# A fused state-space and gated feed-forward layer: x tile 0 loaded as two halves, the second chunk's x in one transfer, and the up projection's column halves in one stretch

## The chip, the core and the metric

The kernel runs on one core of one Trainium2 chip. The metric is device time in microseconds, taken over several runs of the same program. The core's engines run side by side, each on its own list of instructions, and wait for each other on semaphores: TensorE (PE; its weight loads are PEld), VectorE (DVE), ScalarE (ACT), GpSimd (POOL) and SyncE (SP). Here SP, ACT and POOL also issue the transfers (DMAs); SPq and ACTq in the profile are their issues.

## The reference

x has 2048 tokens of 512 features, in bfloat16. One layer norm feeds two branches, and everything is added:

```
xn = layernorm(x)
A: Bu = xn @ B_bar.T                      (complex, 512 states)
   h[t] = Lam_bar * h[t-1] + Bu[t]
   a = 2 * Re(h @ C.T) + xn * Dskip
B: b = (silu(xn @ w_gate) * (xn @ w_up)) @ w_down      (inner width 1376)
out = x + a + b
```

Lam_bar and B_bar follow from Lambda, log_dt and B, which are small vectors and two 512x512 matrices.

## The kernel before

**Tiling.** The tokens go in 16 tiles of 128, in four chunks of 512 (`NCH` = 4, `TPC` = 4 tiles per chunk). `xall` holds x, `xnT` the normalized x with features on the partitions, which is what the matmuls read. The inner width 1376 is ten full blocks of 128 (`FT - 1`) and a last one of 96. For each chunk there are gate and up matmuls (`gateup_tile`, line 432), the projection to the states (`bproj_tile`, line 357), the recurrence on DVE (`ssm_ops`: rotate u by tables, scan at line 399, rotate back into `wt`), and the output (`out_chunk`): for each tile of tokens one PSUM bank collects eleven feed-forward matmuls (`out_ffn`, line 513) and eight state matmuls (`out_ssm`, line 522). ACT moves PSUM to SBUF. There are eight PSUM banks.

**Order.** The order on each engine is the order of the program text. TensorE's order is written out at the end of the function; the work of DVE is kept in a list, `backlog`, of pieces with costs. `pump(us)` issues pieces as TensorE's time goes by, and `need(tag)` issues what is left of a tag before TensorE uses it. `multiply` issues the products silu(gate) x up (line 451). Chunk 0 begins in a head that works tile by tile (`head_mm`, line 605), after nine dummy matmuls (line 582); then bproj of chunk 0, the rest of its gate and up, bproj 1, gate/up 1, bproj 2, output 0, gate/up 2, bproj 3, output 1, gate/up 3, output 2, output 3.

**The head.** Tile 0 of x is loaded from SP (line 123), tile 1 from ACT (line 125, after a memset of the same bytes, line 124), tile 2 from SP (128), tile 3 from ACT (129), with the first groups of `wg` and `wu` between them (`load_w1`, line 112). The second chunk's x follows from SP in two transfers of two tiles (137). For each tile DVE takes statistics (lines 185, 186; for tiles 1 and 3 lines 612 and 627), ACT makes the inverse deviation (190, 191), DVE normalizes (203), TensorE transposes (220), and DVE or ACT copies the result into `xnT` (227, 229). Before tile 0 is normalized, DVE takes the statistics of tile 1; before tile 2 is normalized, those of tile 3.

**Later layer norms.** `ln_rest(c, on_act)` gives the pieces for chunk c: four statistics, a power on POOL (195), a small product nb on DVE (198), four normalizations (for chunks 2 and 3 on ACT, line 208), each followed by a transposing DMA from SP (234). For chunk 3 the normalized tile is `xn_end`.

**The last block of 96.** Its gate columns and 32 of its up columns form one matmul of 128 columns (`w_last`, line 458, 96 gate and 32 up). The other 64 up columns (`wu_last`) fill half the columns of the array, so two chunks run side by side: for each of four k, a matmul into the upper and one into the lower half of a bank (line 468). This is done for chunks 0 and 1 in gate/up 1, and for chunks 2 and 3 in gate/up 3. ACT copies the halves to `ul` (471), and a product fills `gu_last` (473), of which there are two buffers.

**Output.** For chunks 0 to 2 ACT copies a bank to `res` (529) and POOL adds it to the output in memory (530). Before that SP copies x of these chunks to the output (734). `skip_op` and `skip_store` (490, 496) add xn x Dskip.

Of the kernel before, what the change touches and what calls it, by code (L numbers as in the profile page):

```python
# [11 lines left out]
BF16 = mybir.dt.bfloat16  # L12
ALU = mybir.AluOpType
ACT = mybir.ActivationFunctionType
# [9 lines left out]
def kernel(  # L24
# [17 lines left out]
    nc = tc.nc  # L42
    _, L, D = A_x.shape
# [15 lines left out]
    LA, LB = 32, 64  # L59
# [13 lines left out]
    def bank(shape=(128, CW), dtype=F32):  # L73
        return psum.tile(list(shape), dtype, name="ps")
# [4 lines left out]
    x_v = A_x[0].rearrange("(n p) d -> p n d", p=128)  # L79
    out_v = out[0].rearrange("(n p) d -> p n d", p=128)  # L80
# [4 lines left out]
    xall = const.tile([128, NT, D], BF16, name="xall")  # L85
    xnT = const.tile([128, KD, L], BF16, name="xnT")
# [8 lines left out]
    wu_last = const.tile([128, KD, LB], BF16, name="wu_last")  # L95
    wd_sb = const.tile([128, FT, D], BF16, name="wd_sb")
# [5 lines left out]
    CF = const.tile([128, 2, NQ, D], BF16, name="CF")  # L102
# [7 lines left out]
    def load_w1(q, tiles, view, gi):  # L110
        a, b = fgroups[gi]
        q.dma_start(out=tiles[gi][:], in_=view[:, :, a * 128:min(F, b * 128)])
# [6 lines left out]

    nc.scalar.preload_act_table_set("natural_log_exp_and_others")  # L120


    nc.sync.dma_start(out=xall[:, 0, :], in_=x_v[:, 0, :])
    nc.vector.memset(xall[:, 1, 0:D // 2], 0.0)
    nc.scalar.dma_start(out=xall[:, 1, :], in_=x_v[:, 1, :])
    load_w1(nc.sync, wg_g, wg_v, 0)
    load_w1(nc.scalar, wu_g, wu_v, 0)
# [37 lines left out]

    gu_last = [const.tile([128, CW], BF16, name=f"gu_last{i}") for i in range(2)]
    for t in (gu_last[0][LB + LA:128, :], gu_last[1][LB + LA:128, :], wd_sb[LB + LA:128, FT - 1, :]):
        nc.vector.memset(t, 0.0)  # L170


# [74 lines left out]
    V = nc.vector  # L247
# [177 lines left out]
    gu_tiles = {}  # L425
    u_pair = {}
    products = []
# [24 lines left out]

    up_last = {}

    def gateup_last(c):
        ps = bank()
        for k in range(KD):
            nc.tensor.matmul(ps[:], lhsT=w_last[:, k, :], rhs=xnT[:, k, c * CW:(c + 1) * CW],  # L458
                             start=(k == 0), stop=(k == KD - 1))
        u = up_last[c] = up_p.tile([128, CW], BF16, name="ul", bufs=2)  # L460
        nc.scalar.activation(out=gu_last[c % 2][0:LB + LA, :], in_=ps[0:LB + LA], func=ACT.Silu)
        nc.scalar.copy(out=u[LB:LB + LA, :], in_=ps[LB + LA:128])
        if c % 2 == 0:
            return
        ps = bank()
        for k in range(KD):
            for i in range(2):
                nc.tensor.matmul(ps[i * LB:(i + 1) * LB], lhsT=wu_last[:, k, :],  # L468
                                 rhs=xnT[:, k, (c - 1 + i) * CW:(c + i) * CW], start=(k == 0), stop=(k == KD - 1))
# [29 lines left out]
    o_tiles = {}  # L499

    def out_blocks(n):

        return ((0, D // 2), (D // 2, D - 128), (D - 128, D)) if n == NT - 1 else ((0, D),)

    def out_ffn(n):
        c, i = divmod(n, TPC)
        o_tiles[n] = []
        for lo, hi in out_blocks(n):
            o = bank((128, hi - lo))
            o_tiles[n].append(o)  # L510
            for fi in range(FT):
                t = gu_last[c % 2] if fi == FT - 1 else gu_tiles[c][:, fi, :]
                nc.tensor.matmul(o[:], lhsT=t[:, i * 128:(i + 1) * 128], rhs=wd_sb[:, fi, lo:hi],  # L513
                                 start=(fi == 0), stop=False)

    def out_ssm(n):
        c, i = divmod(n, TPC)
        res = opool.tile([128, D], BF16, name="res")
        for o, (lo, hi) in zip(o_tiles[n], out_blocks(n)):
            for part in range(2):  # L520
                for q in range(NQ):
                    nc.tensor.matmul(o[:], lhsT=w_tiles[c][:, part, q, i * 128:(i + 1) * 128],  # L522
                                     rhs=CF[:, part, q, lo:hi], start=False, stop=(part == 1 and q == NQ - 1))
            if c == NCH - 1:
                V.tensor_tensor(out=res[:, lo:hi], in0=o[:], in1=xn_end[:, i, lo:hi], op=ALU.add)  # L525
                for a, b in ((0, D // 2), (D // 2, D)) if i == 0 else ((lo, hi),):
                    (nc.sync if b == D else nc.scalar).dma_start(out=out_v[:, n, a:b], in_=res[:, a:b])
            else:
                nc.scalar.copy(out=res[:, lo:hi], in_=o[:])  # L529
                nc.gpsimd.dma_start(out=out_v[:, n, lo:hi], in_=res[:, lo:hi], accum_op=ALU.add)  # L530

# [52 lines left out]
    def ln_rest(c, on_act):  # L584
        ops = [(0.7, lambda n=n: ln_stats(n)) for n in range(c * TPC, (c + 1) * TPC)]
        def fin():
            ln_rstd(c * TPC, (c + 1) * TPC)
        def nbf():
            ln_nb(c * TPC, (c + 1) * TPC)
        ops += [(0.1, fin)]  # L590
        tail = [(0.1, nbf)] if on_act else []
        for n in range(c * TPC, (c + 1) * TPC):
            def one(n=n):
                (norm_act if on_act else norm_dve)(n)
                xT_dma(n)
            tail.append((0.05 if on_act else 0.35, one))
        return ops, tail
# [88 lines left out]
    def spread(ops, others, tag, tag2):  # L686

        others = list(others)
        for op in ops:
            queue(tag, [op])  # L690
            if others:
                queue(tag2, [others.pop(0)])

    def queue_ssm(c):
        fwd, back = ssm_ops(c)
# [46 lines left out]
    queue_ssm(3)  # L742
    out_chunk(1)
    gateup_chunk(3)
    out_chunk(2)
    need("skip")
    out_chunk(3)
# [30 lines left out]
```

## Time and profile before

| | |
|---|---|
| runs | 179.62 us median of 3 (179.45 to 179.9) |
| profiled execution | 179.41 us, span 177.6 us |
| granted TensorE clock | 1.0 |
| transfers in all | 15.53 MB, mean 87 GB/s |
| in slices of 4.44 us, the first five | 157, 320, 265, 234, 146 GB/s |
| line 432, gate and up | 37.6 and 37.5 us of TensorE |
| line 513, feed-forward output | 37.2 us |
| line 357 and line 522 | 28.2 and 28.1 us |
| line 468, the 64-column halves | 16 matmuls, 2.1 us |

The span is the time from the first to the last instruction of the program; the profiled execution's own time is 1.8 us more. Busy time of a matmul is modelled and overlaps that of the next, so the spacing of starts says more than the mean of one. The largest single waits of other engines are those of POOL for results (87.2 us) and of ACT for output banks (38.4 us), which is idle time of engines that TensorE does not wait for at that point. Some transfers of the head, from issue to landing: x tiles 0 and 1 took 2.1 and 2.3 us, x tiles 2 and 3 4.5 us each, the first groups of wg and wu 3.9 and 4.6 us, their second groups 4.9 and 5.0 us, and the two transfers of the second chunk's x 5.2 and 4.1 us.

### The profile page before, as it was taken

To read this page: it belongs to the slowest core of one execution; us is meant where nothing else is said; L and a number is where in the kernel's file an instruction comes from. 1 tells how busy PE (TensorE), PEld (TensorE's weight loads), DVE (VectorE), ACT (ScalarE), POOL (GpSimd) and SP (SyncE) were. 2 spreads that over 40 slices of the span, in tenths; PEclk is the share of its full clock that TensorE was granted. 3 is DMA by queue.
4 is the path that set the end of the run, shared out by engine and by line. 5 is a ranking of instruction groups with operands and counts; after the bars stand their busy time and mean duration, and the time that the engine had idled before them with its cause. 6 is when DMAs were issued, how large, how long until landed. Compare 5 with 4: busy or idle time off the path is not lost.

```text
span 177.6 us, 2450 instructions
## 1 busy us (share of the span) xinstructions
PE 172.7 (97%) x900; PEld 83.1 (47%) x916; DVE 154.2 (87%) x237; ACT 94.3 (53%) x173; POOL 23.2 (13%) x29
## 2 busy tenths in 40 slices
PE   8999999999999999999999999999999999999993
PEld 2784444444444444444444444444444444444743
DVE  6789997999999999999999999999999999940033
ACT  4589696978499965033997660024866600220000
POOL 6003000001300000029000000013505000150000
PEclk9999999999999999999999999999999999999999
DMA  5998948993146400022820000007276900072012
GB/s 157 320 265 234 146 95 232 350 140 89 30 87 208 181 0 0 0 30 29 122 61 0 0 0 0 4 2 85 30 119 94 147 0 0 0 87 32 4 49 69
DMA packets 29131, 15.53 MB, mean 87 GB/s; under 512 B 18848, under 2 KB 29056, under 8 KB 29088
## 3 DMA queue, kind: packets, MB, share of 16 engines
q1 hardware_dynamic: 24416, 11.41, 28.3%
q0 software_dynamic: 3456, 3.28, 13.9%
q10 hardware_dynamic: 1248, 0.69, 1.4%
q8 instruction: 7, 0.11, 0.3%
q14 instruction: 4, 0.03, 0.1%
HBM read 8.03 MB, written 5.24 MB: 75 GB/s over the span
## 4 chain that ended last, share of the span: by engine, by line
PE 95%; DVE 1%; DMA 1%; issue 1%
PE ps L432 36%; PE ps L513 21%; PE ps L357 15%; PE ps L522 15%; PE ps L605 3%; PE ps L458 2%; DMA xall<-in_A_x_dram 1%; PE ps L468 1%; PE ps L220 1%; DVE stats L185 0%; DVE stats L612 0%; DVE xall L203 0%; DVE res L525 0%; PE ps L582 0%; DVE mv L186 0%
## 5 line engine op out<-in xcount | busy, mean ns | idle before, releaser
L432 PE MATMUL ps<-xnT,wg 128*128 128x512 bf16 x143 | 37.6, 379 | 0.3
L432 PE MATMUL ps<-xnT,wu 128*128 128x512 bf16 x146 | 37.5, 379 | 0.1
L513 PE MATMUL ps<-wd_sb,guT 128*128 128x512 bf16 (+2 forms) x177 | 37.2, 355 | 0.2
L399 DVE TENSOR_TENSOR_SCAN g<-r_t,car,u 128x512 bf16<-128x512 f32 x24 | 28.9, 1266 | 0.0
L522 PE MATMUL ps<-CF,wt 128*128 128x512 bf16 (+2 forms) x140 | 28.1, 355 | 0.2
L357 PE MATMUL ps<-xnT,BT 128*128 128x512 bf16 x126 | 28.2, 379 | 0.1
L529 ACT CAST res<-ps 128x512 bf16<-128x512 f32 x12 | 7.0, 585 | 38.4 <-PE ps L522 38.4
L446 ACT ACTIVATE guT<-ps 128x512 bf16<-128x512 f32 x40 | 24.8, 620 | 3.8 <-PE ps L432 3.7
L447 ACT CAST u<-ps 128x512 bf16<-128x512 f32 x40 | 24.2, 604 | 4.1 <-PE ps L432 4.0
L513 PEld LDWEIGHTS <-guT 128*128 128x128 bf16 x180 | 16.9, 98 | 18.0
L432 PEld LDWEIGHTS <-wu 128*128 128x128 bf16 x148 | 14.5, 98 | 17.5
L432 PEld LDWEIGHTS <-wg 128*128 128x128 bf16 x148 | 14.3, 98 | 17.6 <-issue 0.8
L530 POOL DMA_DIRECT2D out_dram<-res x12 | 11.1, 998 | 87.2 <-ACT res L529 87.2
L522 PEld LDWEIGHTS <-wt 128*128 128x128 bf16 x144 | 13.5, 98 | 14.2
L357 PEld LDWEIGHTS <-BT 128*128 128x128 bf16 x128 | 12.5, 98 | 15.1
L359 ACT CAST u<-ps 128x512 bf16<-128x512 f32 x32 | 17.5, 589 | 3.1 <-PE ps L357 3.0
L525 DVE TENSOR_TENSOR res<-ps,xn_end 128x512 bf16<-128x512 f32 (+2 forms) x6 | 3.0, 514 | 14.5 <-PE ps L522 14.5
L451 DVE TENSOR_TENSOR guT<-guT,u 128x1024 bf16<-128x1024 bf16 x20 | 13.5, 680 | 0.0
L367 DVE TENSOR_TENSOR pm<-u,c 128x2048 bf16<-128x2048 bf16 x8 | 9.8, 1221 | 1.2 <-ACT c L284 1.1
L195 POOL TENSOR_TENSOR rstd<-ve,neg_half 128x4 f32<-128x4 f32 x3 | 5.2, 1749 | 40.2 <-DVE ve L194 40.2
L185 DVE BATCH_NORM_STATS2 stats<-xall 128x6 f32<-128x512 bf16 x14 | 9.4, 671 | 1.1 <-DMA xall<-in_A_x_dram 1.1
L367 DVE TENSOR_TENSOR pm<-g,c 128x2048 bf16<-128x2048 bf16 x8 | 9.7, 1218 | 0.1
(108 smaller groups left out, 166.1 us busy)
## 6 DMA issues: line engine op xcount, KB each, us to landing
out_dram<-in_A_x_dram SPq DMA_DIRECT2D x1, 1536.0 KB, 8.9
out_dram<-res POOLq DMA_DIRECT2D x12, 128.0 KB, 3.1
out_dram<-xall POOLq DMA_DIRECT2D x3, 512.0 KB, 5.7
wd_sb<-in_B_w_down_dram SPq DMA_DIRECT2D x1, 1280.0 KB, 10.3
xall<-in_A_x_dram SPq DMA_DIRECT2D x1, 1024.0 KB, 6.3
xall<-in_A_x_dram SPq DMA_DIRECT2D x2, 256.0 KB, 4.6
wg<-in_B_w_gate_dram SPq DMA_DIRECT2D x1, 512.0 KB, 5.2
wu<-in_B_w_up_dram SPq DMA_DIRECT2D x1, 512.0 KB, 6.1
```

Source lines behind the costliest of these rows:

```text
L185: nc.vector.bn_stats(out=stats[:, n, :], in_=xall[:, n, :])
L357: nc.tensor.matmul(ps[:], lhsT=BT[:, part, k, q * 128:(q + 1) * 128], rhs=xnT[:, k, c * CW:(c + 1) * CW], start=(k == 0), stop=(k == KD - 1))
L359: nc.scalar.copy(out=u_tiles[c][:, part, q, :], in_=ps[:])
L367: V.tensor_tensor(out=t[:], in0=flat(src()[:, i]), in1=flat(tab[:]), op=ALU.mult)
L399: V.tensor_tensor_scan(out=g()[:, part, q, :], data0=r_t[:, q:q + 1].to_broadcast([128, CW]), data1=u_tiles[c][:, part, q, :], initial=ini ...
L432: nc.tensor.matmul(ps[:fs, lo:hi], lhsT=wslice(groups, fi, k), rhs=xnT[:, k, c * CW + lo:c * CW + hi], start=(k == 0), stop=(k == KD - 1))
L446: nc.scalar.activation(out=guT[:fs, fi, :], in_=psg[:fs], func=ACT.Silu)
L447: nc.scalar.copy(out=u_pair[c][:fs, fi % 2, :], in_=psu[:fs])
L451: products.append(lambda: V.tensor_tensor(out=g, in0=g, in1=u, op=ALU.mult))
L513: nc.tensor.matmul(o[:], lhsT=t[:, i * 128:(i + 1) * 128], rhs=wd_sb[:, fi, lo:hi], start=(fi == 0), stop=False)
L522: nc.tensor.matmul(o[:], lhsT=w_tiles[c][:, part, q, i * 128:(i + 1) * 128], rhs=CF[:, part, q, lo:hi], start=False, stop=(part == 1 and q ...
L530: nc.gpsimd.dma_start(out=out_v[:, n, lo:hi], in_=res[:, lo:hi], accum_op=ALU.add)
```

## The change

x tile 0 is loaded as two halves of 64 tokens, one from SP and one from ACT; the memset ahead of tile 1 goes. The second chunk's x comes in one transfer. The 64 up columns of the last block are done for all four chunks in one stretch, `up_halves`, which stands in the output of chunk 0, behind its ten feed-forward matmuls per tile. For this the layer norm of chunk 3 moves ahead, among the pieces of chunk 0's recurrence (`spread` now takes a list of tags), and `need("ln3")` stands before the stretch. The eleventh feed-forward matmul of chunk 0's tiles (`out_last`) then needs a product that is not there yet, so it is done in `out_end`, in gate/up 2, after its block 0, and the four result copies and accumulations of chunk 0 (`out_leave`) go with it. `gu_last` gets a third buffer and `ul` has four.

```diff
-    nc.sync.dma_start(out=xall[:, 0, :], in_=x_v[:, 0, :])
-    nc.vector.memset(xall[:, 1, 0:D // 2], 0.0)
+    nc.sync.dma_start(out=xall[0:64, 0, :], in_=x_v[0:64, 0, :])
+    nc.scalar.dma_start(out=xall[64:128, 0, :], in_=x_v[64:128, 0, :])
     nc.scalar.dma_start(out=xall[:, 1, :], in_=x_v[:, 1, :])
...
-    for n in (TPC, TPC + 2):
-        nc.sync.dma_start(out=xall[:, n:n + 2, :], in_=x_v[:, n:n + 2, :])
+    nc.sync.dma_start(out=xall[:, TPC:2 * TPC, :], in_=x_v[:, TPC:2 * TPC, :])
...
+    def product_last(c):
+        g, u = gu_last[c % 3][0:LB + LA, :], ul(c)[0:LB + LA, :]
+        products.append(lambda: V.tensor_tensor(out=g, in0=g, in1=u, op=ALU.mult))
+
+    def up_halves():
+        pss = []
+        for c in range(0, NCH, 2):
+            ps = bank()
+            pss.append(ps)
+            for k in range(KD):
+                for i in range(2):
+                    nc.tensor.matmul(ps[i * LB:(i + 1) * LB], lhsT=wu_last[:, k, :],
+                                     rhs=xnT[:, k, (c + i) * CW:(c + i + 1) * CW], start=(k == 0), stop=(k == KD - 1))
+        for c in range(NCH):
+            i = c % 2
+            nc.scalar.copy(out=ul(c)[0:LB, :], in_=pss[c // 2][i * LB:(i + 1) * LB])
+        product_last(0)
+        product_last(1)
...
-        if c % 2 == 0:
-            return
-        ps = bank()
-        for k in range(KD):
-            for i in range(2):
-                nc.tensor.matmul(ps[i * LB:(i + 1) * LB], lhsT=wu_last[:, k, :],
-                                 rhs=xnT[:, k, (c - 1 + i) * CW:(c + i) * CW], start=(k == 0), stop=(k == KD - 1))
-        for i in range(2):
-            nc.scalar.copy(out=up_last[c - 1 + i][0:LB, :], in_=ps[i * LB:(i + 1) * LB])
-            g, u = gu_last[(c - 1 + i) % 2][0:LB + LA, :], up_last[c - 1 + i][0:LB + LA, :]
-            products.append(lambda g=g, u=u: V.tensor_tensor(out=g, in0=g, in1=u, op=ALU.mult))
+        if c > 1:
+            product_last(c)
...
-            for fi in range(FT):
-                t = gu_last[c % 2] if fi == FT - 1 else gu_tiles[c][:, fi, :]
-                nc.tensor.matmul(o[:], lhsT=t[:, i * 128:(i + 1) * 128], rhs=wd_sb[:, fi, lo:hi],
+            for fi in range(FT - 1):
+                nc.tensor.matmul(o[:], lhsT=gu_tiles[c][:, fi, i * 128:(i + 1) * 128], rhs=wd_sb[:, fi, lo:hi],
                                  start=(fi == 0), stop=False)
+            if c > 0:
+                out_last(n, o, lo, hi, False)
...
+            if c == 2 and fi == 0:
+                out_end(0)
...
+        if c == 0:
+            need("ln3")
+            up_halves()
+            multiply(0)
         need(f"ssm{c}")
...
+    def out_end(c):
+        for n in range(c * TPC, (c + 1) * TPC):
+            o = o_tiles[n][0]
+            out_last(n, o, 0, D, True)
+            out_leave(n, o, opool.tile([128, D], BF16, name="res"))
...
+    stats3, norm3 = ln_rest(3, True)
     queue("ln2", stats2)
     queue("ssm0", fwd0[6:8])
-    spread(fwd0[8:] + back0, norm2, "ssm0", "ln2")
+    spread(fwd0[8:] + back0, norm2 + stats3 + norm3, "ssm0",
+           ["ln2"] * len(norm2) + ["ln3"] * (len(stats3) + len(norm3)))
...
-    stats3, norm3 = ln_rest(3, True)
-    queue("ssm1", fwd1[0:6])
-    queue("ln3", stats3)
-    queue("ssm1", fwd1[6:8])
-    spread(fwd1[8:] + back1, norm3, "ssm1", "ln3")
+    queue("ssm1", fwd1 + back1)
```

More of the change, by code (lines that the diff above doesn't have):

```diff
@@ L164 @@
     nc.gpsimd.iota(out=jidx[:], pattern=[[1, CW]], base=0, channel_multiplier=0, allow_small_or_imprecise_dtypes=True)
-    gu_last = [const.tile([128, CW], BF16, name=f"gu_last{i}") for i in range(2)]
-    for t in (gu_last[0][LB + LA:128, :], gu_last[1][LB + LA:128, :], wd_sb[LB + LA:128, FT - 1, :]):
+    gu_last = [const.tile([128, CW], BF16, name=f"gu_last{i}") for i in range(3)]
+    for t in (*(g[LB + LA:128, :] for g in gu_last), wd_sb[LB + LA:128, FT - 1, :]):
         nc.vector.memset(t, 0.0)
@@ L453, with ul @@
     up_last = {}
+    def ul(c):
+        if c not in up_last:
+            up_last[c] = up_p.tile([128, CW], BF16, name="ul", bufs=4)
+        return up_last[c]
+    def product_last(c):
[15 more added lines that the diff above has]
+        product_last(1)
     def gateup_last(c):
@@ L459, in gateup_last @@
                              start=(k == 0), stop=(k == KD - 1))
[L460 to L461 removed]
+        u = ul(c)
+        nc.scalar.activation(out=gu_last[c % 3][0:LB + LA, :], in_=ps[0:LB + LA], func=ACT.Silu)
         nc.scalar.copy(out=u[LB:LB + LA, :], in_=ps[LB + LA:128])
[L463 to L473 removed]
+        if c > 1:
+            product_last(c)
     def gateup_tile(c, fi):
@@ L510, in out_ffn, with out_last @@
             o_tiles[n].append(o)
-            for fi in range(FT):
-                t = gu_last[c % 2] if fi == FT - 1 else gu_tiles[c][:, fi, :]
-                nc.tensor.matmul(o[:], lhsT=t[:, i * 128:(i + 1) * 128], rhs=wd_sb[:, fi, lo:hi],
+            for fi in range(FT - 1):
+                nc.tensor.matmul(o[:], lhsT=gu_tiles[c][:, fi, i * 128:(i + 1) * 128], rhs=wd_sb[:, fi, lo:hi],
                                  start=(fi == 0), stop=False)
+            if c > 0:
+                out_last(n, o, lo, hi, False)
+    def out_last(n, o, lo, hi, stop):
+        c, i = divmod(n, TPC)
+        nc.tensor.matmul(o[:], lhsT=gu_last[c % 3][:, i * 128:(i + 1) * 128], rhs=wd_sb[:, FT - 1, lo:hi],
+                         start=False, stop=stop)
     def out_ssm(n):
         c, i = divmod(n, TPC)
-        res = opool.tile([128, D], BF16, name="res")
+        if c > 0:
+            res = opool.tile([128, D], BF16, name="res")
         for o, (lo, hi) in zip(o_tiles[n], out_blocks(n)):
@@ L522, in out_ssm @@
                     nc.tensor.matmul(o[:], lhsT=w_tiles[c][:, part, q, i * 128:(i + 1) * 128],
-                                     rhs=CF[:, part, q, lo:hi], start=False, stop=(part == 1 and q == NQ - 1))
+                                     rhs=CF[:, part, q, lo:hi], start=False, stop=(c > 0 and part == 1 and q == NQ - 1))
             if c == NCH - 1:
@@ L527, in out_ssm, with out_leave @@
                     (nc.sync if b == D else nc.scalar).dma_start(out=out_v[:, n, a:b], in_=res[:, a:b])
-            else:
-                nc.scalar.copy(out=res[:, lo:hi], in_=o[:])
-                nc.gpsimd.dma_start(out=out_v[:, n, lo:hi], in_=res[:, lo:hi], accum_op=ALU.add)
+            elif c > 0:
+                out_leave(n, o, res)
+    def out_leave(n, o, res):
+        nc.scalar.copy(out=res[:], in_=o[:])
+        nc.gpsimd.dma_start(out=out_v[:, n, :], in_=res[:], accum_op=ALU.add)
     backlog = []
@@ L684, in out_chunk, with spread @@
             pump(2 * NQ * 0.2163)
-    def spread(ops, others, tag, tag2):
-        others = list(others)
+    def out_end(c):
[3 more added lines that the diff above has]
+            out_leave(n, o, opool.tile([128, D], BF16, name="res"))
+    def spread(ops, others, tag, tags):
+        others = list(zip(others, tags))
         for op in ops:
@@ L691, in spread @@
             if others:
-                queue(tag2, [others.pop(0)])
+                op, t = others.pop(0)
+                queue(t, [op])
+        for op, t in others:
+            queue(t, [op])
     def queue_ssm(c):
```

## The prediction

> **What bounds the kernel now.** I read the shares of busy time first, then the chain that ended last, then the timeline of the first 22 us by engine, and last TensorE's own timeline around the place that the change rebuilds.
>
> ```profile
> span 177.6 us, 2450 instructions
> PE 172.7 (97%) x900; PEld 83.1 (47%) x916; DVE 154.2 (87%) x237; ACT 94.3 (53%) x173; POOL 23.2 (13%) x29
> ...
> PE 95%; DVE 1%; DMA 1%; issue 1%
> ```
>
> TensorE is the chain for 95% of the span. In its own waits only two entries stand, 0.8 us at the start and 0.4 us for the first normalized tile (L220 for L203). So anything on DVE, ACT, POOL or a queue counts only if it makes TensorE wait, and a gain has to come from TensorE's idle time in the head or from its own work.
>
> The head, where TensorE still waits for data (start, duration, engine, line):
>
> ```profile
> 0.74 0.39 SPq L123 DMA_DIRECT2D xall<-in_A_x_dram  x1
> ...
> 1.10 0.43 ACTq L125 DMA_DIRECT2D xall<-in_A_x_dram  x1
> ...
> 1.19 0.42 SPq L112 DMA_DIRECT2D wg<-in_B_w_gate_dram  x1
> ...
> 2.04 0.53 ACTq L129 DMA_DIRECT2D xall<-in_A_x_dram  x1
> ...
> 2.81 0.69 DVE L185 BATCH_NORM_STATS2 stats<-xall 128x6 f32<-128x512 bf16 x1 [0.75 <-DMA xall<-in_A_x_dram]
> ...
> 6.15 0.69 DVE L185 BATCH_NORM_STATS2 stats<-xall 128x6 f32<-128x512 bf16 x1 [0.31 <-DMA xall<-in_A_x_dram]
> ...
> 6.98 0.66 DVE L627 BATCH_NORM_STATS2 stats<-xall 128x6 f32<-128x512 bf16 x1
> ...
> 7.66 0.41 DVE L203 TENSOR_SCALAR xall<-xall,mv,rstd 128x512 bf16<-128x512 bf16 x1
> ...
> 8.13 0.23 PEld L220 LDWEIGHTS <-xall 128*128 128x128 bf16 x4 [0.26 <-DVE xall L203]
> ```
>
> Tile 0 starts the chain (landing 2.1 us after its issue at 0.74), but it does not fix TensorE's pace. At 8.13 TensorE waits again, for the normalization of tile 2 (DVE, 7.66 to 8.07). DVE does that after the statistics of tile 3 (6.98 to 7.64), and these come after the statistics of tile 2, which waited for tile 2's landing (issued 1.65, landed 4.5 us later). From 8.13 on TensorE has no idle time to its last matmul but the switches below. So what counts at the head is the time of this one normalization, and tiles 2 and 3 set it.
>
> The second place is the column stretch, on TensorE alone:
>
> ```profile
> 38.52 1.03 PE L458 MATMUL ps<-xnT,w_last 128*128 128x512 bf16 x4
> 39.48 1.05 PE L468 MATMUL ps<-xnT,wu_last 128*64 128x512 bf16 x8
> 40.47 1.04 PE L432 MATMUL ps<-xnT,wg 128*128 128x512 bf16 x4
> ```
>
> A 128x512 matmul follows the next at 0.216 us (the chain gives "0.86 PE ps L458 x4"). Four of them before the stretch take 39.48 - 38.52 = 0.96 instead of 0.86; the stretch's eight halves run as four pairs and take 0.99 instead of 0.86. One stretch so costs 0.10 + 0.12 = 0.22 us of switching, and there are two, here and at 123.45.
>
> **The change, part by part.** *One column stretch instead of two.* Sixteen halves as eight pairs in one stretch, the same matmuls otherwise: -0.22 us on TensorE, the engine that sets the end. Between its two banks there is no other shape, so no new switch; bounds 0.17 (a longer switch at a new place) to 0.25.
>
> *Its new place.* TensorE runs 0.98 us earlier from 39.5 to the end of the first output chunk's feed-forward part (40 matmuls instead of 44, 63.83 to 72.47); the stretch takes 8 x 0.216 + 0.22 = 1.95, and L522 of chunk 0 starts at 74.4 (before: 74.31). Four things are newly due there.
> (a) The last chunk's xnT at the second bank, 73.4. Its statistics are put between chunk 0's scans and rotations on DVE. From 43.44, by the row pitches: 8 scans 9.0, 4 statistics 3.2, carry 0.5, three half rotations 3.5, three products 1.8, then wt's subtraction 1.25 gives 62.8; nb there waits for POOL's power (1.9, as at 80.20) until 63.7. ACT waits for nb in front of its queue from about 60.3; behind it stand bproj evacuations of chunk 2, whose banks are wanted only from 70.3 on, and are free by 65 to 70. Four normalizations at 0.72 with the casts and the c-scalings between them end at 69.1; the transpose on SP takes 1.2 to issue and lands 2.4 us from issue: 71.6. Margin 1.8.
> (b) CF and wt for L522: wt 67.5, then eight CF at 0.67 to 0.74, paced by ACT's scalings: 73.4, the last wanted at 75.9. Margin 2.5.
> (c) The products of gu_last for chunk 0: after chunk 1's rotation (7.2) at 80.6 to 81.0, wanted at 83.9 by the four late matmuls. Margin 3. These four move by themselves, 0.86 us as before.
> (d) Banks: chunk 0's four output banks are held until 84.8, and ACT then makes the four result copies together (2.0). In the built order the gate and up tiles behind them take the banks of the stretch and of the last tile, free since about 78 and 84. No wait.
> On SP the base copy of x to the output goes behind the last chunk's transposes, from 54.4 to about 70.4, and lands 8.9 us later, 79.3; the first accumulation now comes at 85. POOL's broadcast load of Dskip goes behind the third power, to 64; it is used at 124.4. DVE then runs about 1 us later than before into chunk 1, whose result it had finished at 97.8 for a use at 115.8. I cost all of this at nothing; uncovered, each microsecond past a margin is a microsecond of the end.
>
> *Tile 0 as two halves.* Each half has its own issue, at 0.74 on SP and about 0.75 on ACT (the memset that held ACT's first issue to 1.10 goes). The tile lands between 2.5 (half of the bytes per queue) and 2.8 (as now). Worth on the path: nothing to 0.14. TensorE would reach the wait at 8.13 sooner, and that wait's idle time is 8.13 - 7.88 - 0.11 = 0.14 (start of the last matmul before it, and its 0.11). I take nothing.
>
> *What the halves push away.* The built order shows the price: DMA completions use eight semaphores in turn, so a ninth transfer waits until the first has landed. Before, the ninth was the second chunk's first x transfer (3.23 us, no delay). Now it is x tile 3 on ACT: issued at 2.04 before, and now only when the first half has landed, 2.5 to 2.8. Behind it on ACT stands only the first variance chain, due later. But on SP wg's second group (issued 2.20, landed 4.9 later: 7.1) now goes ahead, and wu's (2.68 + 5.0 = 7.7) about ties. Tile 3 landed at 2.04 + 4.5 = 6.5, and DVE wants it at 6.98. Bounds of its landing: 6.5 if its own queue carries it past them, loss 0; 7.7 if it goes last, loss 7.72 - 6.98 = 0.74. Between them: issue 2.65 with the 4.5 to 5.0 of its neighbours gives 7.15 to 7.65, and its packets are larger than wu's and stand alone on their queue, so I take the lower part, 7.25: loss 0.27, call it 0.25. It goes straight into L203 at 7.66 and TensorE at 8.13.
>
> *Second chunk's x in one transfer.* Waits for wg's first group (landed 5.1) as the second of the two did; its bytes follow at once on a queue that is still busy until 7.7. It lands by about 10.0 (9.2 before) for statistics at 11.22. The next issues stay at 5.6 and 6.1. The matmuls of wu's third group want it at 12.6 and it landed at 6.14 + 6.1 = 12.24: cover 0.4, which also limits any head gain to about that.
>
> **The sum.** -0.22 + 0.25 = +0.03 us. The profiled execution took 179.41 (span 177.6 and 1.8 around it) and becomes 179.44; the median of the runs is 0.21 above it, so 179.62 + 0.03 = 179.65.
>
> The Trainium skill, "DMA: Bandwidth & Descriptors", section "Rules for kernel authors", speaks against the halves: two transfers to disjoint partition halves serialize on the same sixteen engines, and one 128-partition transfer should be used. By that rule the first half lands no sooner than the whole tile did, and the third rival below is what follows.
>
> **The rivals.** *Tile 3 is in time.* Its queue is its own and it lands by 6.98: only the switch counts, 179.40. For it: its statistics had 0.4 us of slack. Against: wu's first group, issued on ACT at 1.55, landed after 6.1, no sooner than tile 2 issued later on SP, so a queue of one's own gave no precedence.
> *The head gains.* Tiles 2 and 3 and wu's first group all land 0.4 earlier, since less is in flight (the second chunk's 256 KB no longer start at 3.23). The normalization at 7.66 moves by 0.4, as far as the cover of wu allows: -0.62, 179.0. Against: that transfer was issued last and lands last (8.4).
> *Tile 3 goes last.* The half lands at 2.8, tile 3 is issued behind all of wu's second group and lands at 7.7: -0.22 + 0.74 = +0.52, 180.15.
> *Tile 1 falls behind wg (the slower side).* Before, x tile 1 was issued 0.09 us ahead of wg's first group (1.10, 1.19); now it follows a half on ACT, at about 1.2, a tie. Its statistics (L612) stand ahead of tile 0's normalization on DVE. Halfway between its landing of 3.4 and wg's 5.1, 4.25, L612 moves from 3.64 to 4.27 and L203 by 0.63; 0.19 of it is taken up by the idle 0.14 ahead of 8.13 and 0.05 ahead of 6.20: +0.44, and with tile 3's loss not adding but the larger of both counting, up to +1.3 at the full 5.1. With the switch: +0.2 to +1.1, middle 180.3. It decides from a landing of about 3.9 on.
> *The middle stalls.* nb of the last chunk comes over 1.8 us late, the stretch waits, price about 1 us: 180.4. Against it are three margins of 1.8 to 3.
>
> **How the numbers follow.** Chances: forecast 0.42, tile 3 in time 0.20, head gains 0.11, tile 3 last 0.12, tile 1 late 0.10, middle 0.05. The range 179.1 to 180.3 leaves out about half of the head's gain and the far parts of the last two. 0.3%, about what a measurement of this kernel can tell from no change, is 0.54 us: faster are the head's gain and little else, 0.13; slower are most of the last two and the upper half of tile 3 last, 0.22; the rest 0.65.
>
> **What would show it.** One column stretch of sixteen, at about 72.5, with TensorE's spacing of 0.10 and 0.12 around it once. Tile 3's issue near 2.65 on ACT and its statistics late, with L203 moving from 7.66 to about 7.9 and L220 from 8.13 to 8.4; if L220 stands at 8.1 or before, the in-time rival holds. Statistics of tile 1 later than 3.9 show the slower side. A TensorE wait at the stretch or at the first L522 shows the middle. The forecast is wrong if TensorE idles anywhere after 8.4 apart from that stretch.

## The result, and the profile after

| | before | after |
|---|---|---|
| runs of one comparison | 179.5 us median of 7 (179.3 to 179.9) | 180.8 us median of 7 (180.76 to 182.28) |
| profiled execution, and its span | 179.41, 177.6 | 180.76, 179.0 |
| start of the last matmul in the trace | 174.56 | 175.80 |

By the medians the changed kernel is slower by 1.3 us; the ratio, 1.0092 (interval 1.0069 to 1.0116), stands for more, since it weighs in two runs far above the other five. Its runs fall into two groups, five at 180.76 to 180.82 and two at 182.2 and 182.28; the profiled execution belongs to the lower one, and so does all that is said here unless the upper one is named, and two disturbed runs of the later comparisons (264.81 of the kernel before, 375.74 of one variant) are left out. The kernel before in each later comparison was between 179.42 and 179.58.

The page of the changed kernel, busy time by engine:

```profile
PE 172.7 (96%) x900; PEld 83.3 (47%) x916; DVE 154.3 (86%) x237; ACT 94.6 (53%) x173; POOL 23.2 (13%) x29
```

TensorE is busy for exactly as long as before, 172.7 us, in a span that is 1.4 longer. So the time is idle time of TensorE. Its waits (line, for what, total, times, longest) name one place, where 0.4 stood before:

```profile
PE ps L218 <- DVE xall L201: 1.7, 1, 1.7
PE ps L606 <- PEq L800: 0.8, 1, 0.8
```

The head of the changed kernel, to be laid beside the one shown before (start, duration, engine, line):

```profile
0.74 0.58 SPq L122 DMA_DIRECT2D xall<-in_A_x_dram  x1
...
0.77 0.56 ACTq L123 DMA_DIRECT2D xall<-in_A_x_dram  x1
...
1.37 0.85 ACTq L124 DMA_DIRECT2D xall<-in_A_x_dram  x1
1.37 0.57 SPq L112 DMA_DIRECT2D wg<-in_B_w_gate_dram  x1
...
2.97 0.39 ACTq L128 DMA_DIRECT2D xall<-in_A_x_dram  x1
...
5.35 0.69 DVE L636 BATCH_NORM_STATS2 stats<-xall 128x6 f32<-128x512 bf16 x1 [1.18 <-DMA xall<-in_A_x_dram]
...
5.96 0.40 DVE L201 TENSOR_SCALAR xall<-xall,mv,rstd 128x512 bf16<-128x512 bf16 x1
...
6.41 0.40 PE L218 MATMUL ps<-ident,xall 128*128 128x128 bf16 x4 [1.66 <-DVE xall L201]
...
9.61 0.39 PE L218 MATMUL ps<-ident,xall 128*128 128x128 bf16 x4
```

Read it from the end. Tile 2's transposes start at 9.61 instead of 8.13 and do not wait there: TensorE was already late. Tile 0's transposes (6.41 instead of 4.80) waited for its normalization at 5.96. That could not start at 4.7, when tile 0's deviation was ready, because tile 1's statistics (L636) stand ahead of it on DVE, and these waited until 5.35 for x tile 1. Tile 1 landed at 5.32, 4.0 us after its issue at 1.37; before, it was issued at 1.10 and landed at 3.43. The chain that ended last says the same in one entry (start, length, what):

```profile
1.37 3.96 DMA xall<-in_A_x_dram
```

The rebuilt stretch on TensorE's own timeline:

```profile
71.28 2.54 PE L526 MATMUL ps<-wd_sb,guT 128*128 128x512 bf16 x11
73.75 1.92 PE L470 MATMUL ps<-xnT,wu_last 128*64 128x512 bf16 x16
75.60 2.12 PE L543 MATMUL ps<-CF,wt 128*128 128x512 bf16 x8
```

Eleven matmuls take 73.75 - 71.28 = 2.47 instead of 11 x 0.216 = 2.38, the eight pairs 1.85 instead of 1.73: one switch in and one out, 0.09 and 0.12, and no wait. The rest adds up: the head loses 1.48 (9.61 for 8.13, by the matmuls' starts), the stretch saves 0.22, which is +1.26; the last matmul starts 1.24 later.

### The profile page after: what moved, and what is told of

It is laid out like the page before. It is cut to its first block, busy times and chain, and to the rows that moved or that the text cites. A ratio compares the mean times of both kernels' runs of the same rounds, so it can differ in the third digit from the quotient of the medians.

```text
span 179.0 us, 2450 instructions
## 1 busy us (share of the span) xinstructions
PE 172.7 (96%) x900; PEld 83.3 (47%) x916; DVE 154.3 (86%) x237; ACT 94.6 (53%) x173; POOL 23.2 (13%) x29
## 3 DMA queue, kind: packets, MB, share of 16 engines
HBM read 8.03 MB, written 5.24 MB: 74 GB/s over the span
## 4 chain that ended last, share of the span: by engine, by line
PE 94%; DMA 2%; issue 1%; DVE 0%; ACT 0%
PE ps L430 35%; PE ps L526 19%; PE ps L543 16%; PE ps L355 15%; PE ps L629 3%; DMA xall<-in_A_x_dram 2%; PE ps L481 2%; PE ps L533 2%; PE ps L470 1%; PE ps L218 1%; ACT L120 0%; DVE xall L201 0%; DVE res L546 0%; PE ps L606 0%; PE ps L248 0%
## 5 line engine op out<-in xcount | busy, mean ns | idle before, releaser
L526 PE MATMUL ps<-wd_sb,guT 128*128 128x512 bf16 (+2 forms) x177 | 36.7, 355 | 0.2
L554 POOL DMA_DIRECT2D out_dram<-res x12 | 10.5, 1041 | 78.1 <-ACT res L553 78.1
```

What stands on the lines that cost most here:

```text
L526: nc.tensor.matmul(o[:], lhsT=gu_tiles[c][:, fi, i * 128:(i + 1) * 128], rhs=wd_sb[:, fi, lo:hi], start=(fi == 0), stop=False)
L554: nc.gpsimd.dma_start(out=out_v[:, n, :], in_=res[:], accum_op=ALU.add)
```

## The experiments

Diffs are against the changed kernel unless it says otherwise. Every time is the median of its runs; the ratio is to the kernel before in the same comparison.

**The parts alone.** First the stretch without the two edits of the loads:

```diff
-    nc.sync.dma_start(out=xall[0:64, 0, :], in_=x_v[0:64, 0, :])
-    nc.scalar.dma_start(out=xall[64:128, 0, :], in_=x_v[64:128, 0, :])
+    nc.sync.dma_start(out=xall[:, 0, :], in_=x_v[:, 0, :])
+    nc.vector.memset(xall[:, 1, 0:D // 2], 0.0)
...
-    nc.sync.dma_start(out=xall[:, TPC:2 * TPC, :], in_=x_v[:, TPC:2 * TPC, :])
+    for n in (TPC, TPC + 2):
+        nc.sync.dma_start(out=xall[:, n:n + 2, :], in_=x_v[:, n:n + 2, :])
```

> Only the one column stretch with what it moves; both load edits undone. Theory (tile 1's late landing is the whole loss): tile 1's statistics start at about 3.6 us again, the head is as before, and the kernel is 0.22 us faster than before (ratio about 0.9988). Rival (the stretch or its new order costs part of it): 0.2 us slower or more, with TensorE idle somewhere after 8.2 us.

Measured 179.23 against 179.42, ratio 0.9987 (0.9977 to 0.9998), that is -0.23 us (-0.41 to -0.04). Its stretch runs from 72.49 to 74.34, 1.26 us earlier in the span than in the changed kernel and of the same length.

The saving is real, though its interval nearly reaches nothing, and the loads lose the rest. Of all versions here this is the only one that is faster than the kernel before.

Then the halves alone, in the kernel before (diff against that):

```diff
-    nc.sync.dma_start(out=xall[:, 0, :], in_=x_v[:, 0, :])
-    nc.vector.memset(xall[:, 1, 0:D // 2], 0.0)
+    nc.sync.dma_start(out=xall[0:64, 0, :], in_=x_v[0:64, 0, :])
+    nc.scalar.dma_start(out=xall[64:128, 0, :], in_=x_v[64:128, 0, :])
     nc.scalar.dma_start(out=xall[:, 1, :], in_=x_v[:, 1, :])
```

> Only tile 0 as two halves without the memset, on the kernel before; the second chunk's x stays in two transfers and both column stretches stay. Theory: tile 1 lands near 5.3 us, its statistics and the normalization of tile 0 slip by about 1.6 us, and the kernel is about 1.45 us slower than before (ratio about 1.008). Rival (it takes the merged transfer or the moved stretch as well): under 0.7 us slower.

Measured 182.18 (181.29 to 182.86), ratio 1.0145 (1.0114 to 1.0177): even more than the whole change, in runs that are far apart. In its profile, x tile 1 is issued at 1.38 and lands at 5.24, and tile 0's transposes start at 6.33, all as in the changed kernel. On top of that TensorE runs at half speed afterwards (its timeline; then for stretches of the span their length, TensorE's busy time and matmuls, the granted clock, the DMA share and GB/s):

```profile
6.33 0.40 PE L220 MATMUL ps<-ident,xall 128*128 128x128 bf16 x4 [1.86 <-DVE xall L203]
...
7.89 1.06 PE L605 MATMUL ps<-xnT,wu 128*128 128x128 bf16 x8
```

```profile
6.00:7.00 1.00, 0.63 (x9) 1.00 1.20 254
7.50:8.50 1.00, 1.00 (x13) 0.50 1.10 315
...
11.00:12.00 1.00, 1.00 (x16) 1.00 1.11 352
```

The granted clock falls to 0.50 from 7.43 to 10.84, and eight 128-column matmuls take 1.06 us where the changed kernel's profile has 0.61. Before it fell TensorE had been idle for 1.86 us. So the profile of this run, one of the three upper ones (182.76 to 182.86), holds two losses, the late tile and the clock. The three lower runs, 181.29 to 181.59, lie 0.3 to 0.6 above the first alone (179.5 + 1.5 = 181.0), which is not explained.

The merge alone, in the kernel before:

```diff
-    for n in (TPC, TPC + 2):
-        nc.sync.dma_start(out=xall[:, n:n + 2, :], in_=x_v[:, n:n + 2, :])
+    nc.sync.dma_start(out=xall[:, TPC:2 * TPC, :], in_=x_v[:, TPC:2 * TPC, :])
```

> Only the second chunk's x in one transfer, on the kernel before. Theory: no change, within 0.15 us of before, since its data are wanted only at about 11.2 us. Rival (the merged transfer, or the semaphore turn that it shifts, delays later weights): 0.3 us slower or more, with TensorE waiting for wu's third group near 12.4 us or for BT near 22 us.

Measured 179.82, ratio 1.0022 (1.0013 to 1.0032): +0.4 us, a miss. The time is the rival's, but neither of the rival's waits is there. Timeline of its head:

```profile
3.24 0.54 SPq L136 DMA_DIRECT2D xall<-in_A_x_dram  x1
...
6.56 0.70 DVE L184 BATCH_NORM_STATS2 stats<-xall 128x6 f32<-128x512 bf16 x1 [0.61 <-DMA xall<-in_A_x_dram]
...
8.54 0.23 PEld L219 LDWEIGHTS <-xall 128*128 128x128 bf16 x4 [0.41 <-DVE xall L202]
```

Here all 512 KB are issued at 3.24, behind tile 0's landing at 2.90; before, half of them were and half waited until 5.12. x tile 2 lands at 6.54 (6.13 before), and everything from its statistics to tile 2's transposes is 0.4 late. In the changed kernel the same transfer is issued only at 5.51 and no wait of TensorE goes back to it, so this loss does not seem to be in its 1.3 us. The kernel with both the stretch and the merge, and tile 0 and the memset as before:

> The changed kernel with x tile 0's load and the memset as before; the one stretch and the merged transfer stay. If the parts add: 179.2 (stretch alone) plus 0.4 (merge alone) = 179.6 (179.5 to 179.8), with x tile 2 landing at 6.4 to 6.6. If the merge's cost belongs to the kernel with two stretches only: 179.2.

Measured 179.49, ratio 1.0001 (0.9988 to 1.0013). Against the stretch alone (0.9987) that is +0.25 us for the merge, but the two intervals overlap. Its profile has x tile 2 in by 5.7 and no wait for tile 2. So the merge's cost is clear of the noise only in the kernel before, and that it always comes through tile 2 is not shown.

**What makes tile 1 late.** Three orders of the loads that leave all else alone. In the first, x tile 1 goes on SP, directly behind the first half:

```diff
-    nc.scalar.dma_start(out=xall[:, 1, :], in_=x_v[:, 1, :])
+    nc.sync.dma_start(out=xall[:, 1, :], in_=x_v[:, 1, :])
```

> The changed kernel with x tile 1 issued on SP directly behind the first half, ahead of wg's first group; the halves and all else stay. Theory (what costs is that tile 1 is served behind wg's 256 KB): tile 1 lands by about 4.0 us, its statistics follow tile 0's at about 4.1, and most of the loss goes: between 0.1 us faster and 0.5 us slower than before. Rival (the halves themselves cost, by landing later): tile 0's statistics stay at 3.26 us or later and the kernel stays 1 us or more slower.

Measured 180.55 (180.16 to 182.51), ratio 1.0078 (1.005 to 1.0106): 1.1 us slower than before, beyond the theory's 0.5 and as much as the rival said. The profiled run is the slowest of the nine, 182.51, with a granted clock of 0.50 from 7.60 to 11.01. In its timeline:

```profile
1.98 0.43 SPq L112 DMA_DIRECT2D wg<-in_B_w_gate_dram  x1
...
5.27 0.40 PE L218 MATMUL ps<-ident,xall 128*128 128x128 bf16 x4 [0.72 <-DVE xall L201]
...
7.43 0.91 PE L629 MATMUL ps<-xnT,wg 128*128 128x128 bf16 x8 [1.53 <-DMA wg<-in_B_w_gate_dram]
```

x tile 1, issued on SP at 1.37, lands at 4.12 and tile 0's transposes come 1.14 sooner, close to what was expected. But wg's first group now stands behind wu's (issued at 1.36 on ACT), lands at 7.38 instead of 5.49, and TensorE waits 1.53 us for it. In this run the loss has only changed its place; the halves' later landing, the rival's cause (tile 0's statistics start at 3.29), is not ruled out as a part of it.

In the second, DVE normalizes tile 0 before it looks at tile 1:

```diff
-    nc.vector.bn_stats(out=stats[:, 1, :], in_=xall[:, 1, :])
     norm_dve(0)
+    nc.vector.bn_stats(out=stats[:, 1, :], in_=xall[:, 1, :])
```

> The changed kernel, with tile 0's normalization put ahead of tile 1's first statistics on VectorE (L201 before L636), all loads as they are. Theory (x tile 1's landing at 5.3 sets the whole head through VectorE's order): tile 0's transposes start at 5.2 instead of 6.41, but tile 1's statistics still start at 5.35 and tile 1's normalization at 6.7 instead of 7.04, so tile 2's transposes come about 0.3 earlier than 9.61 and the time is 180.5 (180.3 to 180.7). Rival (what was lost is only the 1.6 us for which TensorE waits for tile 0, as the chain of waits says): most of 1.2 us comes back, 179.6 to 179.8.

Measured 180.61, 180.62, 181.09, 182.01 and 182.28 in five runs, ratio 1.0106 (1.0072 to 1.014). The lowest two lie where the theory put them, the median above; none comes near the rival's. The profiled one (180.62) has tile 0's transposes at 5.23 and its last matmul 0.17 earlier than the changed kernel, not the 1.2 by which the transposes moved:

```profile
5.23 0.48 PE L218 MATMUL ps<-ident,xall 128*128 128x128 bf16 x4 [0.45 <-DVE xall L201]
5.37 0.69 DVE L637 BATCH_NORM_STATS2 stats<-xall 128x6 f32<-128x512 bf16 x1 [0.21 <-DMA xall<-in_A_x_dram]
...
6.88 0.41 DVE L201 TENSOR_SCALAR xall<-xall,mv,rstd 128x512 bf16<-128x512 bf16 x1 [0.42 <-ACT rstd L189]
```

Tile 1's own normalization is still at 6.88 (7.04 in the changed kernel). Nor is tile 0 quite free of tile 1: TensorE now waits for DVE's copy of tile 0's transposes, which stands behind tile 1's statistics.

```profile
PE ps L629 <- DVE xnT L225: 0.6, 1, 0.6
```

So the one wait that the list of waits names is not the price; tile 1's landing is, whichever tile is made to wait for it.

In the third, both halves go on SP and x tile 1 is the first on ACT:

```diff
-    nc.scalar.dma_start(out=xall[64:128, 0, :], in_=x_v[64:128, 0, :])
+    nc.sync.dma_start(out=xall[64:128, 0, :], in_=x_v[64:128, 0, :])
```

> The changed kernel with both halves of x tile 0 on SP's queue, so that x tile 1 is the first on ACT's. Theory (x tile 1's place on its queue costs, the halves themselves only what tile 0 lands later): x tile 1 is issued at 0.8 and lands by 3.6; tile 0's second half is issued at 1.3 and lands at 3.1 to 3.4; tile 0's transposes start at 5.2 to 5.4 and the time is 179.6 to 180.1. Rival (splitting a tile by its tokens is what costs, on whatever queue): tile 0's second half lands after 4.0 and the time is 180.6 or more.

Measured 183.31 (182.49 to 183.81), ratio 1.0203 (1.0178 to 1.0228): the theory as I put it failed by more than 3 us, and both signs of the rival are there.

```profile
0.77 0.39 ACTq L124 DMA_DIRECT2D xall<-in_A_x_dram  x1
...
1.19 0.45 ACTq L112 DMA_DIRECT2D wu<-in_B_w_up_dram  x1
...
1.37 0.58 SPq L123 DMA_DIRECT2D xall<-in_A_x_dram  x1
...
4.92 0.69 DVE L183 BATCH_NORM_STATS2 stats<-xall 128x6 f32<-128x512 bf16 x1 [2.72 <-DMA xall<-in_A_x_dram]
...
7.73 1.06 PE L629 MATMUL ps<-xnT,wg 128*128 128x128 bf16 x8
```

x tile 1 is in at 2.99, but the second half, issued at 1.37 on a queue of its own, lands at 4.82, behind the 256 KB of wu that ACT issued at 1.19 and that landed at 4.42. And after 2.1 us without work on TensorE the matmuls run at half speed until 12.4 (1.06 us for eight). Two things to explain, then: why a half takes 0.58 to issue, and why a transfer waits for an earlier one of another queue.

**Issue, or order?** With tile 0 whole on SP and no memset, x tile 1 is the first on ACT:

```diff
-    nc.sync.dma_start(out=xall[0:64, 0, :], in_=x_v[0:64, 0, :])
-    nc.scalar.dma_start(out=xall[64:128, 0, :], in_=x_v[64:128, 0, :])
+    nc.sync.dma_start(out=xall[:, 0, :], in_=x_v[:, 0, :])
```

> The changed kernel with x tile 0 in one transfer on SP again, and without the memset that the kernel before had ahead of x tile 1 on ACT's queue; the merged transfer and the one stretch stay. Theory: x tile 1 is issued at 0.8 beside x tile 0 and lands by 3.5, before its statistics are due; tile 2's transposes come at 8.1 plus at most 0.45 for the merged transfer (which alone cost 0.4), and the time is the stretch alone's 179.2 plus 0.2 to 0.4, 179.4 to 179.6. Rival (the memset kept the two first issues apart, and without it both take 0.58 and everything behind them is late): x tile 0 lands at 3.0 to 3.2 and the time is 179.8 to 180.2. If the halves were not the cause, it stays at 180.8.

Measured 179.93, ratio 1.0028 (1.0007 to 1.0049), in the rival's range, with a cause that neither had: the two issues take 0.40 and 0.39 side by side, but tile 0 lands at 3.40 and tile 1 at 3.59. The kernel with the stretch, the merge and the memset differs from this one by the memset alone: there tile 0 lands at 2.96 and its transposes start at 4.96, here at 5.41, and the medians are 0.44 apart as well. So two queues at once do not make an issue slow; the 64 partitions are left as the cause, which the next run tests.

Cut by columns, each half has 128 partitions:

```diff
-    nc.sync.dma_start(out=xall[0:64, 0, :], in_=x_v[0:64, 0, :])
-    nc.scalar.dma_start(out=xall[64:128, 0, :], in_=x_v[64:128, 0, :])
+    nc.sync.dma_start(out=xall[:, 0, 0:D // 2], in_=x_v[:, 0, 0:D // 2])
+    nc.scalar.dma_start(out=xall[:, 0, D // 2:D], in_=x_v[:, 0, D // 2:D])
```

> The changed kernel with x tile 0 cut by columns instead of tokens: 128 partitions x 256 on SP, 128 x 256 on ACT. Theory (a transfer of 64 partitions takes 0.57 us to issue and the next one on its queue as long or longer; one of 128 partitions takes 0.4): both halves issue in 0.4 to 0.45, x tile 1 is issued at 1.2, lands by 4.0, and the time is the merged transfer's and the one stretch's, 179.5 to 180.0. Rival (whatever cut, x tile 1 stands second on ACT's queue, beside wg's first group): it lands after 4.8 and the time is 180.5 or more.

Measured 180.39 (180.18 to 181.7), ratio 1.0063 (1.0038 to 1.0087). On the issue the theory was right, on the landing the rival, whose time was 0.1 too long:

```profile
0.77 0.40 ACTq L123 DMA_DIRECT2D xall<-in_A_x_dram  x1
...
1.20 0.46 ACTq L124 DMA_DIRECT2D xall<-in_A_x_dram  x1
1.20 0.42 SPq L112 DMA_DIRECT2D wg<-in_B_w_gate_dram  x1
...
5.11 0.69 DVE L636 BATCH_NORM_STATS2 stats<-xall 128x6 f32<-128x512 bf16 x1 [1.05 <-DMA xall<-in_A_x_dram]
```

The halves issue in 0.40, x tile 1 is issued at 1.20 and still lands at 5.08, beside wg's first group (4.97), which is issued in the same hundredth. What both cuts have lost is the 0.09 us by which x tile 1 was ahead of wg. How the two transfers shared the way differs: in the changed kernel ACT's queue moved 1 packet between 2.8 and 3.6 us while SP's moved 162; here 116 and 289 moved side by side between 3.2 and 4.0. x tile 1 is late both times. Two runs test the lead by giving it back. SP must wait for memsets on the bytes that wg will fill; the token halves stay:

```diff
+    nc.vector.memset(wg_g[0][:], 0.0)
+    nc.vector.memset(wg_g[0][:, 0:KD // 2, :], 0.0)
     nc.scalar.dma_start(out=xall[:, 1, :], in_=x_v[:, 1, :])
     load_w1(nc.sync, wg_g, wg_v, 0)
```

> The changed kernel (halves of tokens) with memsets of wg's first group on VectorE ahead of its load, so that SP issues it at about 1.7 instead of 1.37, behind x tile 1 on ACT (1.37). Order theory: x tile 1 lands at 3.7 to 4.1 instead of 5.3, tile 0's transposes start at 5.2 to 5.4 instead of 6.41, and the time is 179.5 (one stretch and merged transfer) plus the 0.45 by which tile 0 lands later: 179.8 to 180.1. Rival (halves of 64 partitions slow what follows them): x tile 1 lands after 4.6 and the time stays at 180.5 or more.

Measured 180.12 (four runs at 180.03 to 180.12, three at 181.2 to 181.51), ratio 1.0065 (1.0037 to 1.0092), a shade above the theory's time and landing and well below the rival's:

```profile
1.37 0.85 ACTq L126 DMA_DIRECT2D xall<-in_A_x_dram  x1
...
1.88 0.43 SPq L112 DMA_DIRECT2D wg<-in_B_w_gate_dram  x1
...
4.20 0.69 DVE L638 BATCH_NORM_STATS2 stats<-xall 128x6 f32<-128x512 bf16 x1
...
5.27 0.40 PE L220 MATMUL ps<-ident,xall 128*128 128x128 bf16 x4 [0.79 <-DVE xall L203]
```

x tile 1, issued at the same 1.37, lands at 4.18 instead of 5.32, and wg, issued half a microsecond later, lands at 5.21 instead of 5.49. TensorE has one wait more than the changed kernel, for wu's first group:

```profile
PE ps L631 <- DMA wu<-in_B_w_up_dram: 0.3, 1, 0.3
```

With the halves by columns and one memset:

> The halves by columns (128 partitions x 256 each), with wg's first group held back by one memset to about 1.45, behind x tile 1 on ACT (1.20). Order theory: x tile 1 lands at 3.5 to 4.0 instead of 5.08, tile 0's transposes start at 5.0 to 5.3 instead of 6.17, and the time is 179.5 to 179.9 instead of 180.4. Rival (x tile 1 is late whenever it stands second on its queue): it lands after 4.6, 180.3 or more.

Measured 179.76, ratio 1.0012 (1.0002 to 1.0022): x tile 1 at 3.93, tile 0's transposes at 5.02, all as the theory has it. Side by side (issue and landing in us, the later half where there are two; the last column is the median, and for the second row the lower group):

| tile 0 | x tile 1 issued | wg issued | tile 0 landed | x tile 1 landed | tile 0's transposes | time |
|---|---|---|---|---|---|---|
| whole (before) | 1.10 | 1.19 | 2.79 | 3.43 | 4.80 | 179.5 |
| token halves, wg held | 1.37 | 1.88 | 3.13 | 4.18 | 5.27 | 180.1 |
| token halves (changed kernel) | 1.37 | 1.37 | 3.16 | 5.32 | 6.41 | 180.8 |
| column halves, wg held | 1.20 | 1.49 | 2.80 | 3.93 | 5.02 | 179.76 |
| column halves | 1.20 | 1.20 | 3.05 | 5.08 | 6.17 | 180.39 |
| whole, stretch and merge | 1.09 | 1.20 | 2.96 | 3.54 | 4.96 | 179.49 |

The lost lead is the main price, 0.7 us of 1.3: with a lead of 0.09 or more x tile 1 lands 2.3 to 2.8 after its issue, with none 3.9 to 4.0. (Holding wg moves what is issued behind it too: the second chunk's x goes at 3.93 instead of 5.51.) But a tie is not all of it. With x tile 1 on SP, level with wu's 256 KB on ACT (1.37 and 1.36), x tile 1 landed 2.75 after its issue. And with tile 0 whole and no memset, wg on SP (1.20) landed at 5.22, before wu on ACT at 5.52, though wu was issued first (1.19). So in the traced ties the transfer on ACT came off worse; why, the runs do not show.

What remains with wg held and token halves, 0.6 over the last row, can be followed in the profiles. Tile 0's transposes start 0.31 later than in the last row. Then TensorE waits for wu's first group, which is issued at 2.24, behind the 0.85 that x tile 1's issue takes, instead of at 1.55, and lands at 7.03 instead of 6.11. With this tile 2's transposes start 0.72 later (8.87 for 8.15), and the last matmul too. So the slow issues have a price of their own there. The 0.3 that remains with column halves is not split.

**The clock.** Two runs fill TensorE's idle time ahead of tile 0's transposes:

```diff
-    dummy(9, CW)
+    dummy(17, CW)
```

First in the changed kernel:

> The changed kernel with 17 instead of 9 dummy matmuls ahead of tile 0's transposes, so that TensorE idles about 0.4 us instead of 1.7 before them. Theory (the second mode of the changed kernel's runs, two of seven at 182.2, is the granted clock falling to 0.5 for one step of 3.41 us after the idle stretch): all runs lie within 180.6 to 181.0, none at 182 or above, with the clock at 1.0 throughout. Rival (the second mode has another cause): one run in four or so is still at 182. The median of the lower mode is 180.8 by both.

Measured 181.29 (six runs, 180.9 to 181.57), ratio 1.0093 (1.0074 to 1.0112). No run is at 182, as the theory has it, but six runs of a kernel that gets there two times in seven would miss it once in eight by chance ((5/7) to the sixth is 0.13), and five of the six lie above the theory's 181.0. The record also speaks against the theory: the three upper runs of the halves alone, one of which has the fall in its trace, have a mean granted clock of 0.990 or 0.991, both upper runs of the changed kernel 1.0. A clock that opens late leaves that mean at 1.0, as in the profile with both halves on SP; whether the upper runs had this, no trace shows. Why the six runs spread so far is open too. In the profiled run (180.9) the dummies cost nothing: the transposes start at 6.55, right behind the normalization that ended at 6.50, because x tile 1 landed at 5.47. Until the clock opens dummies are 0.427 apart instead of 0.216, so in other runs they may have ended after the data had come. Then in the kernel before with the halves alone:

> The kernel before with the halves alone, and 17 dummy matmuls instead of 9 ahead of tile 0's transposes. Theory (the halves alone cost the head's 1.5 us, and what they cost above that, 181.3 to 182.9 in six runs, is TensorE's clock after the idle stretch): 180.9 to 181.4, no run above 181.7. Rival (without the merge the halves cost more, by the weights behind them): 181.4 or more in the lowest run.

Measured 181.34 (181.19 to 181.64), ratio 1.0091 (1.0075 to 1.0108), where the same kernel with nine dummies had 181.29 to 182.86. That agrees with the theory: the upper runs are gone. The rival falls only just, its 181.4 being 0.2 above the lowest run. The Trainium skill, "TensorE: Matmul & The Clock Gate", "Part 1: The HAM clock gate", has TensorE at half rate until some 3.4 us of activity, judged in windows that run by themselves, and back there after an idle window of that length. The half rate and the length of the dip agree (0.50 for 3.41 us); but in the halves' profile 1.86 us of idle time, within one step of 3.41, came before the fall, and in the changed kernel's 1.66 us brought none. What put two runs of the changed kernel at 182.2 stays open.

## Why the prediction was wrong

The forecast was 179.65 within 179.1 to 180.3, no change the likeliest; it is 180.8. Step by step:

- **What bounds the kernel: right in kind.** Only the head's idle time and the stretch counted. That tile 0 "does not fix TensorE's pace" and tiles 2 and 3 do was true only of the trace it was read from, where tile 1 was in time.
- **One stretch instead of two: right.** -0.22 put; 0.09 and 0.12 of switching in the trace, -0.23 (-0.41 to -0.04) alone.
- **Its new place: right.** No wait of TensorE after the head. The last chunk's transposes are issued at 66.1 to 70.4 and land by 72.8 for a use at 74.6, with 1.8 to spare, as put; the accumulations come at 86.7, behind the base copy's landing at 78.5.
- **"Tile 0 as two halves": the step that failed.** It priced the halves' landing (2.5 to 2.8) and took nothing. The halves landed at 2.95 and 3.16, the whole tile at 2.79 before. Over all profiles with these halves on two queues the first lands at 2.88 to 3.05 and the second at 3.13 to 3.21; the whole tile, with the memset, lands at 2.79 to 2.96. So the tile is complete 0.2 to 0.4 later, which goes with an issue that takes 0.57 instead of 0.39, and no row of before shows that. Above all the step put at nothing what stood behind the half on ACT: x tile 1, issued at 1.37 in a tie with wg, landed 1.9 later than before, and with it the head lost 1.48. The Trainium skill, "DMA: Bandwidth & Descriptors", "Rules for kernel authors", says that two transfers to disjoint partition halves serialize and advises one transfer of 128 partitions; these landings agree with the advice. That the first half lands no sooner is the prediction's own step from it, and so is the way to slower (tile 3 last), which is not the one that happened.
- **The rival "tile 1 falls behind wg" was the case**, with its place and its sign named (statistics of tile 1 later than 3.9; they start at 5.35), at a chance of 0.10. Its top was a landing at 5.1 and +1.1; measured 5.32 and +1.3. Its middle reckoned the lateness as a landing halfway between the two transfers (4.25). The runs show no halfway: 3.4 with a lead of 0.09, 5.1 to 5.3 without. The text had a row that points to this itself, wu's first group on ACT that landed no sooner than a tile issued later on SP, and used it only for tile 3.
- **"What the halves push away": mechanism right, off the path.** Tile 3 was issued at 2.97, right after the first half's landing at 2.95, as put (2.65), and landed at 7.86 (put: 7.25). But with DVE late it was wanted only at 8.19, so the +0.25 did not arise.
- **The merge: right here, wrong in the kernel before.** It waited for wg's first group (5.51 after 5.49), and no wait of TensorE in the changed kernel goes back to it. Where tile 0 is whole it is issued at 3.24 and costs 0.4; with the one stretch the 0.25 is within the noise.

## What to carry to other kernels

Before a load is put ahead of others on a queue, list every transfer of all queues by the time of its issue, and ask which small, urgent one loses its place to a large one: a lead of 0.3 to 0.5 us moved a landing by 1.1 here, and the time by 0.6 to 0.7; before the change a lead of 0.09 had been enough. A memset that seems to do nothing but delay can be what keeps such an order (0.44 here, with tile 0 whole). And a wait at the first instruction of an engine's chain may hide a second one behind it: try the reordering that removes the named wait alone before believing its price.

## What the runs showed of the hardware that was not expected

- A load of 64 partitions takes 0.56 to 0.59 us to issue, one of 128 partitions with the same bytes (the column half) 0.40, and twice the bytes (the whole tile) 0.39 to 0.40. The transfer issued right behind it on the same queue is slow too: 0.82 to 0.85 instead of 0.43 to 0.46 on ACT, for x tile 1 and, in the run with x tile 1 on SP, for wu; 0.57 instead of 0.42 for wg on SP. Held until 1.88, half a microsecond behind the end of the half's issue, wg took 0.43.
- Transfers of SP's and ACT's queues were served about in the order of issue where 0.09 us or more lay between them, and in the traced ties SP's came off better. With column halves, x tile 1 on ACT and wg's first group on SP issued together, x tile 1 landed last (5.08 after 4.97); with token halves and wg issued 0.5 later, both landed earlier (4.18 and 5.21 instead of 5.32 and 5.49).
- The granted clock can fall to 0.50 for 3.41 us after 1.86 us of idle time (1.66 in the changed kernel's profile brought no fall), which in the halves' profile put tile 2's transposes at 11.09, another 1.5 us behind the changed kernel's 9.61.
